# Two attention blocks and a SwiGLU layer on one core: moving columns taken from two halves in turn, and one more cast on VectorE

## The chip, the cores and the metric

The kernel runs on one core of a Trainium2 chip, in one launch. Time is device time in microseconds (us). Three runs of the kernel before took 1459.44 to 1459.61 us, with a median of 1459.46 us. PE is TensorE's matmul side and PEld its weight loads, DVE is VectorE, ACT is ScalarE, POOL is GpSimd, SP is the engine that issues the DMAs here.

## The reference

The input x has 4 batches of 12,416 tokens of 128 numbers. Attention runs twice: 32 inducing rows look at the tokens, which gives a summary h of 32 rows, and then every token looks at h. The result goes through a gated feed-forward layer with 1,536 inner units.

```
def mab(q, kv):
    s = scale * (q @ kv.transpose(0, 2, 1))
    a = np.exp(s - s.max(-1, keepdims=True))
    a /= a.sum(-1, keepdims=True) + 1e-09
    return a @ kv
h = mab(I, x)
attn = mab(x, h)                  # (4, 12416, 128)

g = attn @ w_gate                 # 49664 tokens, 128 -> 1536
val = attn @ w_val
out = (g / (1 + np.exp(-g)) * val) @ w_out
```

## The kernel before

**Columns and steps.** A batch's tokens are cut into 25 columns (`COLS`): 13 of 512 tokens and 12 of 480. Each column takes 12 steps (`NT`), one for each 128 of the 1,536 inner units. One step of one column is a slot, so there are 300 slots in a batch and 1,200 in all. The second attention's last product is folded into the weights: for each batch the kernel multiplies h with the gate and value weights once, in high and low parts, into a tile `tw` (`st.w`), and the moving operand of a column is then a tile `stack` that holds the token's 32 attention weights four times, as high and low parts, which SP's DMAs put there (`spread`, L499).

**One slot.** `front` makes the gate and the value product, two PE matmuls (L691, L692) that both read the same `stack` tile as moving operand, into two PSUM tiles named `gv`. `gate` lets ACT take the silu of the first (L697). `value` lets DVE multiply it with the second (L705); the result h goes to a tile `h`, or back into the PSUM tile for steps 1, 5 and 9 (`DVE_TILES`). `split` makes two fp32r parts of h: the high part `h_hi` is a cast (L713), done by DVE where the step is in `CAST` and by ACT elsewhere; the low part `h_lo` is the difference (L715), done by DVE in the steps of `DVE_TILES` and by POOL elsewhere. `back` makes three matmuls for a step, into one PSUM tile `o` over the 12 steps of a column: `h_hi` with the low part of the output weights (L729), `h_hi` with the high part (L730), and `h_lo` with the high part (L731). After the last step `evac` lets DVE copy `o` out (L738) and SP store it (L740). The first column of the first batch is an exception (`whole`): its h stays in F32, and one F32 product of each step (L727) takes the place of the three.

**Order.** All instructions are written in one fixed order by the loop at L756. In a slot this is: the products of slot k; silu and multiplication of slot k; the split of slot k-1; whatever attention steps of the next batch are due at this slot; and then the three output products of a slot that lies some slots back. The list `pend` and the number `ahead` set how far back: 5 slots in quiet stretches (`SKEW`), up to 10 ahead of a burst (`HI`). In seven slots a burst comes (a long exponential on ACT), and there DVE casts whatever the step is. The attention of the next batch is spread by `plan` over the slots of this batch, so that only the first batch's attention, some 60 us, stands by itself. In the fourth batch nothing is interleaved but the finishing of its own columns.

**Buffers.** `stack` has 3 buffers, `silu` 2, `h` 3, `h_hi` 11, `h_lo` 10, and PSUM has 6 tiles `gv` and 2 tiles `o`. The tiles `stack`, `h_hi` and `h_lo` are 64 elements longer than a column (`WB`), and a column begins at an offset in them that `AT` sets: 16, 48 and 48 elements for the wide columns and 0, 32 and 16 for the narrow ones.

**The moving operand.** In all five products a matmul streams its n columns (512 or 480) in the order in which they lie in SBUF: `st.stack[c][:, :n]`, `u.hi[:, :n]`, `u.lo[:, :n]`. The output of each goes to PSUM in the same order, and the host puts the blocks of tokens back into place.

Of the kernel before, what the change touches and what calls it, by code (L numbers as in the profile page):

```python
# [17 lines left out]
B, N, C, M, DFF = 4, 12416, 128, 32, 1536  # L18
P = 128
NG = 4  # L20
NTB = N // NG // 32


def starts(sizes):
# [10 lines left out]
WF = 32 * max(FC)  # L35
WB = WF + 64
AT = (16, 48, 48), (0, 32, 16)
NT = DFF // P
# [14 lines left out]
WP = 512  # L53
# [1 line left out]
PC = 384  # L55
GA = 4
DVE_TILES = {1, 5, 9}
CAST = {11}
E0 = 36


# [44 lines left out]
def induced_set_attention_then_swiglu(ctx: ExitStack, tc: tile.TileContext, xt, xn, ind, wgv, wo, out):  # L106
    nc = tc.nc
# [44 lines left out]
    def wcol(k, t):  # L152
        at = WP * (t // 2) + 2 * P * k + P * (t % 2)
        return slice(at, at + P)

    wgv_sb = const.tile([P, 2 * DFF], F32, name="wgv_sb")
    wo_hi = const.tile([P, DFF], F32R, name="wo_hi")
    wo_lo = const.tile([P, DFF], F32R, name="wo_lo")
# [39 lines left out]
    def at(u):  # L198

        return AT[u > NG * FC.count(max(FC))]  # L200
# [10 lines left out]
    def attention(b, one, xn0=None, xt0=None):  # L211
# [5 lines left out]
        def psum(second=0):  # L217
            if xn0 is not None or second:
                return ps_gv.tile([P, 512], F32, name="gv")
            return ps_o.tile([P, 512], F32, name="o")  # L220
# [53 lines left out]
        def s1(q, second=0):  # L274
            if q == 0:
                st.s = one.tile([P, NTB * 32], F32, name="s_all")
                st.mx = att.tile([P, NCH], F32, name="mx")
# [84 lines left out]
        def hacc2(q):  # L362
            g = q >= GA
            n0, n1 = (0, CH0[GA])[g], (CH0[GA], NTB)[g]
            if q in (0, GA):
# [65 lines left out]
        def sl2(b0, b1):  # L431
            return st.s2[:, b0:b1, :]

        def s2_m(b0, b1, second=0):
            if not hasattr(st, "s2"):
                st.s2 = one.tile([P, NTB, M], F32, name="s_all")
            st.sp[b0] = psum(second)
# [16 lines left out]

        def exp2(b0=0, b1=NTB):
            nc.scalar.activation(out=sl2(b0, b1), in_=sl2(b0, b1), func=AF.Exp)
# [166 lines left out]
    start = tc.manual_schedule()  # L623
    start.__enter__()
    s_all = oneb.tile([P, NTB * 32], F32, name="s_all")
    with tc.tile_pool(name="xt0", bufs=NCH - NXT) as xt0, tc.tile_pool(name="xn0", bufs=NCH - NXN) as xn0:
        cur = attention(0, one, xn0, xt0)
        f = cur.f
# [3 lines left out]
        pieces = {}  # L632
# [11 lines left out]
        def run(token):  # L644
            name, *args = token.split(":")
            args = [int(x) if x.isdigit() else x for x in args]
            if name == "ld":
                load_piece(*args)
            elif args and args[0] in pieces:
                getattr(pieces[args[0]], name)(*args[1:])  # L650
            else:
                short[name](*args)
# [27 lines left out]
    def front(st, b, c, t):  # L680
        u = Tile()
        q, j = COLS[c]
        u.b, u.q, u.j, u.t = b, q, j, t
        u.at = at(c)
        n = u.n = WF if q == 0 else 32 * FC[q]

        u.whole = b == 0 and c == 0
        rhs = st.stack[c][:, :n]
        u.g = ps_gv.tile([P, 512], F32, name="gv")
        u.v = ps_gv.tile([P, 512], F32, name="gv")  # L690
        nc.tensor.matmul(out=u.g[:, :n], lhsT=st.w[:, wcol(0, t)], rhs=rhs, start=True, stop=True)  # L691
        nc.tensor.matmul(out=u.v[:, :n], lhsT=st.w[:, wcol(1, t)], rhs=rhs, start=True, stop=True)  # L692
        return u
# [5 lines left out]
    def value(u):  # L699
        n = u.n  # L700
        if u.whole:
            u.h = hip.tile([P, WB], F32, name="h_hi")[:, :WF]
        else:
            u.h = u.v if u.t in DVE_TILES else hp.tile([P, WF], F32, name="h")
        nc.vector.tensor_mul(out=u.h[:, :n], in0=u.v[:, :n], in1=u.s[:, :n])  # L705
# [13 lines left out]
    def back(u):  # L719
        n, t = u.n, u.t  # L720
        if t == 0:
            acc["o"] = ps_o.tile([P, 512], F32, name="o")
        o = acc["o"]
        ws = slice(P * t, P * t + P)
        if u.whole:
            k = t % (WP // P)
            nc.tensor.matmul(out=o[:, :n], lhsT=pieces[f"o{t // (WP // P)}"].w[:, P * k:P * k + P], rhs=u.h[:, :n], start=(t == 0), stop=(t == NT - 1))  # L727
        else:
            nc.tensor.matmul(out=o[:, :n], lhsT=wo_lo[:, ws], rhs=u.hi[:, :n], start=(t == 0), stop=False)  # L729
            nc.tensor.matmul(out=o[:, :n], lhsT=wo_hi[:, ws], rhs=u.hi[:, :n], start=False, stop=False)  # L730
            nc.tensor.matmul(out=o[:, :n], lhsT=wo_hi[:, ws], rhs=u.lo[:, :n], start=False, stop=(t == NT - 1))  # L731
        if t == NT - 1:
            evac(u, o)

    def evac(u, o):
        n = u.n
        ob = obp.tile([P, WF], F32, name="ob")
        nc.vector.tensor_copy(out=ob[:, :n], in_=o[:, :n])  # L738
        at = NG * 32 * FC0[u.q] + u.j * n
        nc.sync.dma_start(out=out[u.b, P * at:P * (at + n)].rearrange("(d t) -> d t", d=P), in_=ob[:, :n])  # L740
# [6 lines left out]
    def first(t):  # L747
        made.append(front(cur, 0, 0, t))
        pend.append(made[t])

    short |= dict(f=first, g=lambda t: gate(made[t]), m=lambda t: value(made[t]), k=lambda t: back(pend.pop(0)))
    for token in SECOND.split():
        run(token)
    cur.steps = [(slot, lambda token=token: run(token)) for slot, tokens in FIRST.items() for token in tokens.split()]
    ahead = len(pend)
    for b in range(B):  # L756
        nxt = attention(b + 1, (one, oneb)[(b + 1) % 2]) if b + 1 < B else None
        if nxt is not None:
            nxt.steps = plan(nxt, PA if b == 0 else PB)
            if b == 0:  # L760
                cur.steps.append((nxt.e1, lambda: run(f"e2:52:{NTB}")))
                for q in range(2, NF):
# [6 lines left out]
        for slot in range(NT if b == 0 else 0, SLOTS):  # L769
            c, t = slot // NT, slot % NT  # L770
            u = front(cur, b, c, t)
            gate(u)
            value(u)
            u.cast_dve = t in CAST
            u.last = b == B - 1 and slot == SLOTS - 1
            if wait:
                split(wait[0])
                pend.append(wait.pop(0))
            wait.append(u)
            if slot in bursts:  # L780
                u.cast_dve = True
                split(u)
                pend.append(wait.pop(0))
            for a in (cur, nxt):
                while a is not None and a.steps and a.steps[0][0] <= slot:

                    if pend and pend[0].t in getattr(a.steps[0][1], "acc", ()):
                        break
                    a.steps.pop(0)[1]()
            ahead = min(ahead + 1 / RAMP, HI) if nxt is not None and slot < last_burst else max(ahead - 1 / RAMP, SKEW)  # L790
            if slot in bursts:
                ahead = SKEW - (b == 0)
            while len(pend) + len(wait) > ahead:
                back(pend.pop(0))
# [5 lines left out]
    for u in pend + wait:  # L800
        back(u)
# [37 lines left out]
```

## Time and profile before

| | before |
|---|---|
| median of 3 runs | 1459.46 us |
| the profiled execution, its span | 1459.38 us, 1457.6 us |
| PE busy | 1446.8 us (99%) |
| ACT busy | 1278.5 us (88%) |
| POOL busy | 1208.5 us (83%) |
| DVE busy | 1195.6 us (82%) |
| granted TensorE clock | 1.000 |
| share of PE in the chain that ended last | 94% |

The span is what the profiler sees of the instructions; 1.8 us of the execution's time lie around it. A matmul's busy time is longer than its turn: one follows the next before the first has ended, so the turn (from one start to the next) has to be read from a timeline and not from a mean duration. Granted clock 1.000 means that TensorE was never slowed. The chain of work that ended last follows the execution backwards from its last instruction, each time to what released it.

### The profile page before, as it was taken

How to read it: one execution, taken by the hardware profiler on the slowest of the kernel's cores; microseconds unless marked ns; L12 is line 12 of the kernel's file. 1: busy time of each engine (PE TensorE's matmuls, PEld its weight loads, DVE VectorE, ACT ScalarE, POOL GpSimd, SP SyncE). 2: the span in 40 equal slices, each digit the busy share in tenths (PEclk: the TensorE clock that was granted, in tenths of full speed). 3: DMA queues.
4: the chain of work that ended last, by engine and by line, in shares of the span. 5: the costliest groups of instructions: out<-in, count | busy, mean ns of one | idle time of the engine just before them, and what ended most of it. 6: DMA issues, size and time to landing. Idle time of an engine off the chain costs nothing.

```text
span 1457.6 us, 24926 instructions
## 1 busy us (share of the span) xinstructions
PE 1446.8 (99%) x7452; PEld 1174.3 (81%) x7452; DVE 1195.6 (82%) x2080; ACT 1278.5 (88%) x2388; POOL 1208.5 (83%) x995
## 2 busy tenths in 40 slices
PE   8999999999999999999999999999999999999999
PEld 5577788788887787888888788688888888888887
DVE  6888778887888789888788778987878878878877
ACT  5888898799998887998989888799899999999997
POOL 1689778888998778888899868878889889988987
PEclk9999999999999999999999999999999999999999
DMA  9234522221144242211123522221111111111110
GB/s 370 66 99 127 182 74 99 103 66 54 45 134 138 79 136 105 75 46 41 35 68 114 185 86 87 105 79 42 35 36 41 44 37 37 44 35 40 37 41 21
DMA packets 50822, 119.80 MB, mean 82 GB/s; under 512 B 11392, under 2 KB 28288, under 8 KB 50688
## 3 DMA queue, kind: packets, MB, share of 16 engines
q1 hardware_dynamic: 50688, 118.22, 24.8%
q8 instruction: 59, 0.97, 0.3%
q14 instruction: 75, 0.61, 0.1%
HBM read 62.87 MB, written 25.43 MB: 61 GB/s over the span
## 4 chain that ended last, share of the span: by engine, by line
PE 94%; ACT 2%; DMA 2%; POOL 1%; issue 1%; DVE 0%; SPq 0%; ACTq 0%; DVEq 0%
PE gv L691 18%; PE o L729 18%; PE gv L692 18%; PE o L731 18%; PE o L730 18%; PE gv L270 2%; PE o L318 1%; DMA s_all<-wgv 1%; DMA xt<-xt 1%; PE o L270 1%; PE o L727 1%; ACT silu L697 1%; POOL h_lo L715 1%; ACT h_hi L713 0%; PE gv L420 0%
## 5 line engine op out<-in xcount | busy, mean ns | idle before, releaser
L715 POOL TENSOR_TENSOR h_lo<-h,h_hi 128x512 fp32r<-128x512 f32 (+1 forms) x890 | 1113.2, 1276 | 202.4 <-ACT h_hi L713 142.4
L697 ACT ACTIVATE silu<-gv 128x512 f32<-128x512 f32 (+1 forms) x1200 | 704.2, 588 | 112.5 <-PE gv L691 73.5
L705 DVE TENSOR_TENSOR h<-gv,silu 128x512 f32<-128x512 f32 (+1 forms) x891 | 594.2, 668 | 194.5 <-ACT silu L697 143.8
L713 ACT CAST h_hi<-h 128x512 fp32r<-128x512 f32 (+1 forms) x788 | 475.2, 603 | 29.8 <-DVE h L705 24.6
L691 PE MATMUL gv<-stack,tw 128*128 128x512 f32 (+1 forms) x1200 | 469.0, 391 | 2.0 <-DVE stack L543 1.3
L692 PE MATMUL gv<-stack,tw 128*128 128x512 f32 (+1 forms) x1200 | 463.2, 386 | 0.6 <-ACT silu L697 0.4
L729 PE MATMUL o<-h_hi,wo_lo 128*128 128x512 f32 (+1 forms) x1188 | 460.8, 388 | 0.0
L731 PE MATMUL o<-h_lo,wo_hi 128*128 128x512 f32 (+1 forms) x1188 | 457.6, 385 | 0.0
L730 PE MATMUL o<-h_hi,wo_hi 128*128 128x512 f32 (+1 forms) x1188 | 455.3, 383 | 0.0
L729 PEld LDWEIGHTS o<-h_hi,wo_lo 128*128 128x128 f32 x1188 | 222.6, 187 | 53.9 <-issue 12.1
L691 PEld LDWEIGHTS gv<-stack,tw 128*128 128x128 f32 x1200 | 225.3, 188 | 48.5 <-ACT tw L412 2.6
L692 PEld LDWEIGHTS gv<-stack,tw 128*128 128x128 f32 x1200 | 225.8, 188 | 47.1 <-ACT silu L697 4.0
L731 PEld LDWEIGHTS o<-h_lo,wo_hi 128*128 128x128 f32 x1188 | 223.1, 188 | 42.6 <-POOL h_lo L715 0.4
L730 PEld LDWEIGHTS o<-h_hi,wo_hi 128*128 128x128 f32 x1188 | 223.1, 188 | 41.1
L705 DVE TENSOR_TENSOR gv<-gv,silu 128x512 f32<-128x512 f32 (+1 forms) x297 | 201.7, 679 | 40.5 <-ACT silu L697 39.3
L715 DVE TENSOR_TENSOR h_lo<-gv,h_hi 128x512 fp32r<-128x512 f32 (+1 forms) x297 | 197.5, 665 | 1.8 <-ACT h_hi L713 0.2
L713 ACT CAST h_hi<-gv 128x512 fp32r<-128x512 f32 (+1 forms) x294 | 167.4, 570 | 10.0 <-DVE gv L705 8.8
L738 DVE COPY ob<-o 128x512 f32<-128x512 f32 (+1 forms) x100 | 66.4, 664 | 0.8 <-PE o L731 0.8
L713 DVE CAST h_hi<-h 128x512 fp32r<-128x512 f32 (+1 forms) x103 | 60.6, 589 | 0.0
L483 POOL TENSOR_TENSOR a_lo<-aT,a_hi 128x480 fp32r<-128x480 f32 (+2 forms) x26 | 32.6, 1253 | 0.0
L190 POOL TENSOR_TENSOR wgv_sb<-s_all 128x512 int32<-128x512 int32 x2 | 2.9, 1456 | 28.8 <-ACT s_all L178 28.8
L467 POOL TENSOR_TENSOR s_all<-s_all,sm 128x512 f32<-128x512 f32 (+2 forms) x27 | 26.1, 967 | 0.0
(155 smaller groups left out, 476.5 us busy)
## 6 DMA issues: line engine op xcount, KB each, us to landing
xt_sb<-xt SPq DMA_DIRECT2D x32, 896.0 KB, 5.3
xn_sb<-xn SPq DMA_DIRECT2D x18, 896.0 KB, 5.9
out<-ob SPq DMA_DIRECT2D x52, 256.0 KB, 2.0
out<-ob SPq DMA_DIRECT2D x48, 240.0 KB, 2.0
stack<-a_hi SPq DMA_DIRECT2D x96, 64.0 KB, 2.0
stack<-a_lo SPq DMA_DIRECT2D x96, 64.0 KB, 2.0
stack<-a_hi SPq DMA_DIRECT2D x96, 60.0 KB, 2.0
stack<-a_lo SPq DMA_DIRECT2D x96, 60.0 KB, 2.0
```

The lines of the kernel that those rows point to most:

```text
L270: nc.tensor.matmul(out=ps[32 * j:32 * j + 32, 32 * (lo - b0):32 * (hi - b0)], lhsT=lhsT, rhs=st.xt[q][:, lo - CH0[q]:hi - CH0[q], j, :], s ...
L483: eng.tensor_sub(out=st.al[q][:, :n], in0=st.at[q][:, :n], in1=st.ah[q][:, :n].bitcast(F32))
L691: nc.tensor.matmul(out=u.g[:, :n], lhsT=st.w[:, wcol(0, t)], rhs=rhs, start=True, stop=True)
L692: nc.tensor.matmul(out=u.v[:, :n], lhsT=st.w[:, wcol(1, t)], rhs=rhs, start=True, stop=True)
L697: nc.scalar.activation(out=u.s[:, :u.n], in_=u.g[:, :u.n], func=AF.Silu)
L705: nc.vector.tensor_mul(out=u.h[:, :n], in0=u.v[:, :n], in1=u.s[:, :n])
L713: (nc.vector.tensor_copy if u.cast_dve else nc.scalar.copy)(out=u.hi[:, :n], in_=u.h[:, :n])
L715: eng.tensor_sub(out=u.lo[:, :n], in0=u.h[:, :n], in1=u.hi[:, :n].bitcast(F32))
L729: nc.tensor.matmul(out=o[:, :n], lhsT=wo_lo[:, ws], rhs=u.hi[:, :n], start=(t == 0), stop=False)
L730: nc.tensor.matmul(out=o[:, :n], lhsT=wo_hi[:, ws], rhs=u.hi[:, :n], start=False, stop=False)
L731: nc.tensor.matmul(out=o[:, :n], lhsT=wo_hi[:, ws], rhs=u.lo[:, :n], start=False, stop=(t == NT - 1))
L738: nc.vector.tensor_copy(out=ob[:, :n], in_=o[:, :n])
```

## The change

A helper `turns` gives a view of the same n columns in another order: column 0, column n/2, column 1, column n/2 + 1, and so on. The view has two dimensions beside the partition: n/2 positions one element apart, and within each the two halves, n/2 elements apart (256 elements or 1,024 bytes in a wide column, 240 elements or 960 bytes in a narrow one). The five products of a slot, and the F32 product of the first column, read their moving operand through it. The outputs are written to PSUM as before, one column after the other, so h lies in turned order; the output product turns it once more, and the host undoes both turns with one permutation of every block. No buffer, DMA, offset or weight changes.

Step 3 joins step 11 in `CAST`: DVE makes `h_hi` of step 3, ACT no longer does.

```diff
+def turns(x):
+
+    return x.rearrange("p (a b) -> p b a", a=2)
...
-CAST = {11}
+CAST = {3, 11}
...
-        rhs = st.stack[c][:, :n]
+        rhs = turns(st.stack[c][:, :n])
...
-            nc.tensor.matmul(out=o[:, :n], lhsT=pieces[f"o{t // (WP // P)}"].w[:, P * k:P * k + P], rhs=u.h[:, :n], start=(t == 0), stop=(t == NT - 1))
+            nc.tensor.matmul(out=o[:, :n], lhsT=pieces[f"o{t // (WP // P)}"].w[:, P * k:P * k + P], rhs=turns(u.h[:, :n]), start=(t == 0), stop=(t == NT - 1))
         else:
-            nc.tensor.matmul(out=o[:, :n], lhsT=wo_lo[:, ws], rhs=u.hi[:, :n], start=(t == 0), stop=False)
-            nc.tensor.matmul(out=o[:, :n], lhsT=wo_hi[:, ws], rhs=u.hi[:, :n], start=False, stop=False)
-            nc.tensor.matmul(out=o[:, :n], lhsT=wo_hi[:, ws], rhs=u.lo[:, :n], start=False, stop=(t == NT - 1))
+            hi, lo = turns(u.hi[:, :n]), turns(u.lo[:, :n])
+            nc.tensor.matmul(out=o[:, :n], lhsT=wo_lo[:, ws], rhs=hi, start=(t == 0), stop=False)
+            nc.tensor.matmul(out=o[:, :n], lhsT=wo_hi[:, ws], rhs=hi, start=False, stop=False)
+            nc.tensor.matmul(out=o[:, :n], lhsT=wo_hi[:, ws], rhs=lo, start=False, stop=(t == NT - 1))
...
-        blk = o[:, P * NG * 32 * c0:P * NG * 32 * (c0 + c)]
+        n = WF if c0 == 0 else 32 * c
+        turn = np.arange(n).reshape(2, n // 2).T.reshape(-1)
+        back = np.argsort(turn[turn])
+        blk = o[:, P * NG * 32 * c0:P * NG * 32 * (c0 + c)].reshape(B, -1, P, n)[..., back]
```

## The prediction

> **What bounds the kernel now.** The page comes first: busy time, the slices and the chain of work that ended last.
>
> ```profile
> span 1457.6 us, 24926 instructions
> PE 1446.8 (99%) x7452; PEld 1174.3 (81%) x7452; DVE 1195.6 (82%) x2080; ACT 1278.5 (88%) x2388; POOL 1208.5 (83%) x995
> ...
> PE   8999999999999999999999999999999999999999
> ...
> PE 94%; ACT 2%; DMA 2%; POOL 1%; issue 1%; DVE 0%; SPq 0%; ACTq 0%; DVEq 0%
> ```
>
> PE is busy in every slice, and 94% of the chain is PE following itself. So the time is the number of products times the turn of one, and only a shorter or longer turn moves it. The timeline of PE gives the turns: quiet stretches of the fourth batch (wide, then narrow columns) and of the first batch's narrow columns.
>
> ```profile
> 1200.07 0.39 PE L691 MATMUL gv<-stack,tw 128*128 128x512 f32 x1
> ...
> 1202.34 0.39 PE L691 MATMUL gv<-stack,tw 128*128 128x512 f32 x1
> ```
> ```profile
> 1400.32 0.38 PE L691 MATMUL gv<-stack,tw 128*128 128x480 f32 x1
> 1400.54 0.38 PE L692 MATMUL gv<-stack,tw 128*128 128x480 f32 x1
> 1400.76 0.38 PE L729 MATMUL o<-h_hi,wo_lo 128*128 128x480 f32 x1
> 1400.98 0.38 PE L730 MATMUL o<-h_hi,wo_hi 128*128 128x480 f32 x1
> 1401.19 0.38 PE L731 MATMUL o<-h_lo,wo_hi 128*128 128x480 f32 x1
> 1401.41 0.38 PE L691 MATMUL gv<-stack,tw 128*128 128x480 f32 x1
> ```
> ```profile
> 350.05 0.38 PE L691 MATMUL gv<-stack,tw 128*128 128x480 f32 x1
> ...
> 352.20 0.38 PE L691 MATMUL gv<-stack,tw 128*128 128x480 f32 x1
> ```
>
> Between the two wide rows lie ten products: a wide slot takes 2.27 / 2 = 1.135 us, 0.227 us a product. A narrow slot takes 1.09 us, 0.218 a product, and in the first batch 2.15 / 2 = 1.075. With a sixteenth fewer columns a narrow product should take 0.213 if columns set its time, and one amount of work takes 1.09 in one stretch and 1.075 in another. So a turn holds something beside the columns themselves.
>
> Is there room below? The only other product of this shape is the first column's F32 one, which goes in two passes.
>
> ```profile
> 50.74 1.02 PE L727 MATMUL o<-h_hi,s_all 128*128 128x512 f32 x2
> ```
> ```profile
> L727 PE MATMUL o<-h_hi,s_all x16: 590/592/592, 50.7 to 60.6; 128*128 128x512 f32 x16
> ```
>
> The first fence is the timeline, which merges the two passes; the second is the list of this line's instructions. Two passes of 0.592 us each end 1.02 us after the first began, so the second began 0.43 us later. I read the F32 pass as taking two ticks for a column where the fp32r product takes one (an estimate: no row shows the tick). Then 512 columns at one tick are 0.215 us, and the fp32r turn has 0.012 us over it. Is that the weight load beside it? One place speaks against it:
>
> ```profile
> 209.21 0.39 PE L691 MATMUL gv<-stack,tw 128*128 128x512 f32 x1
> 209.41 0.19 PEld L692 LDWEIGHTS gv<-stack,tw 128*128 128x128 f32 x1 [0.24 <-ACT silu L697]
> 209.43 0.48 PE L692 MATMUL gv<-stack,tw 128*128 128x512 f32 x1
> ```
>
> Here the next weights began to load 0.20 us into the product, and the next product still stands 0.22 to 0.23 behind it. So the excess belongs to the streaming of the moving operand or to the product itself; the change touches the first.
>
> **The turned read, part by part.** It removes no instruction and adds none: 3,084 wide products (624 slots of two, 612 of three) and 2,880 narrow ones (576 slots of five) read the same bytes in another order. No row of before has a moving operand that jumps at every column, so its turn has to be bounded from both sides.
>
> Lower bound: the excess goes wholly. A wide slot becomes 5 x 0.215 = 1.075 us and a narrow one 1.075 x 480 / 512 = 1.008. The gains are 612 x (1.135 - 1.075) = 36.7 us, 480 x (1.09 - 1.008) = 39.4 and 96 x (1.075 - 1.008) = 6.4 (first batch), together 82.5 us. Upper bound: each column is read by itself and costs what it costs in the F32 pass, 0.43 us for 512. Slots become 2.15 and 2.016 us: 612 x 1.015 + 480 x 0.926 + 96 x 0.941 = 621.2 + 444.5 + 90.3 = 1156 us more.
>
> I take the lower end. What decides for me is that the narrow turn isn't one number: from row to row it is 0.22, 0.22, 0.22, 0.21, 0.22, its sum differs between batches, and L729 and L730, which differ in these rows, stream the same h_hi. An excess that changes while bytes, count and operand stay the same is a matter of which addresses meet which, and order of reading changes just that. A fixed toll per product would be the same everywhere.
>
> [...]
>
> **Step 3's cast.** 99 casts (100 columns less the first, which isn't split) go from ACT to DVE. The stretches have their cost:
>
> ```profile
> 1130.00:1290.00 160.00, 160.00 (x707) 132.53 (x706) 131.10 (x216) 147.97 (x271) 142.49 (x112) 1.00 0.13 40
> 1305.00:1445.00 140.00, 140.00 (x642) 120.31 (x641) 113.81 (x192) 126.93 (x246) 121.10 (x101) 1.00 0.11 34
> ```
>
> (The columns are stretch, PE, PEld, DVE, ACT, POOL, clock, DMA.) The groups of L713 in these two stretches, and the waits of the whole span:
>
> ```profile
> L713 ACT CAST h_hi<-h 128x512 fp32r<-128x512 f32 x95 | 58.4, 614 | 2.0 <-DVE h L705 1.7
> ...
> L713 DVE CAST h_hi<-h 128x512 fp32r<-128x512 f32 x12 | 5.0, 420 | 0.0
> ...
> L713 DVE CAST h_hi<-h 128x480 fp32r<-128x480 f32 x11 | 6.6, 600 | 0.0
> ```
> ```profile
> POOL h_lo L715 <- DVE h_hi L713: 16.1, 30, 1.5
> ...
> POOL h_lo L715 <- ACT h_hi L713: 142.4, 216, 8.2
> ```
>
> ACT loses 99 x 0.6 = about 59 us, DVE gains 99 x 0.42 to 0.60 = 42 to 59. On DVE the cast stands behind the multiplication of step 4; behind it stand the multiplication of step 5, and on POOL the low part of step 3. PE needs that low part some five slots later, 5 us, so with PE at its present turn the cast costs nothing. Without that cover it would cost POOL's wait, 16.1 / 30 = 0.54 us each.
>
> **What is late next.** The wide stretch has 141 slots, the narrow one 128. POOL is busy 142.49 / 141 = 1.01 us and 121.10 / 128 = 0.95 us of a slot, DVE 0.93 and 0.89 (0.97 and 0.94 with another twelfth of a cast), ACT 1.05 and 0.99 (1.00 and 0.94 with a cast less). All lie below the new PE slots of 1.075 and 1.008, POOL by 0.06. But POOL also idles 17.5 / 141 = 0.124 and 18.9 / 128 = 0.148 us of a slot, mostly behind casts. If this idling shrinks as needed, the cost is 0. If half of it stays, and each moved cast adds 0.54 / 12 = 0.045, POOL's slots are 1.01 + 0.062 + 0.045 = 1.117 and 0.95 + 0.074 + 0.045 = 1.069, and the gains shrink to 612 x 0.018 + 480 x 0.021 + 96 x 0.006 = 11 + 10 + 1 = 22 us. Between 0 and 60 us given back I take 25, nearer to the first: five slots of lead are there to lend.
>
> **Sum.** Against the profiled execution: 1459.4 - 82.5 + 25 = 1402 us. That execution lies 0.1 us under the median, so nothing is added.
>
> **The rivals.** *The upstream engines set the pace.* PE quickens, and POOL, fed by two casts of DVE, becomes the bound: 1459.4 - 22 = 1437 us. For it: 0.06 us of room a slot. Against it: POOL's wait for ACT's casts, 142.4 us, is idleness PE's pace allowed.
>
> *The order of reading doesn't matter.* The excess is a toll of each fp32r product, or reading is the same speed in any order. Then only the cast moves, under cover: 1459 us. For it: the wide turn is 0.227 at every place that I looked at. Against it: the narrow turns.
>
> *Every column pays for its jump: slower.* [...] At the F32 pass's pace that is 1459.4 + 1156 = 2615 us. It decides from the point at which a column costs more than now, 0.227 / 512 = 0.44 ns. For it: all moving operands of before are neighbours in runs of 32 or more, so the trace has no sign that jumps are free. [...]
>
> **Chances.** The forecast 0.52 (1402, itself 1375 to 1420), POOL's pace 0.15 (1420 to 1450), no matter 0.13 (1455 to 1464), the jump 0.20. The range 1374 to 1465 holds the first three. A difference under 0.2%, 3 us, can't be told from none. Faster: 0.52 + 0.15 = 0.67; same 0.12; slower 0.20 plus 0.01 of the third case.
>
> **What would show it.** If the forecast holds, the timeline's wide turn is near 0.215 us and the narrow one near 0.202, alike in all batches; PE's share of busy time falls below 99% with waits for h_lo; DVE has 99 casts more in L713 and ACT as many fewer. If POOL sets the pace, the turns shorten and PE stands idle ahead of L731 behind L715. If order doesn't matter, turns stay at 0.227 and 0.218. If the jump costs, they are 0.4 or more and ACT, DVE and POOL idle half the time. The forecast is wrong if wide and narrow turns move unlike (1,024 and 960 bytes are different distances), or if the excess sits in the product and not in its read.

## The result and the profile after

The changed kernel takes 1417.3 us (median of 4 runs, 1416.7 to 1418.6) against 1459.5 us: a ratio of 0.971, with a 95% interval of 0.9693 to 0.9727. The forecast was 1402 us, so it is faster, by 42 us where 57 were expected.

The page of the kernel after, first its span and busy times, then its chain of waits:

```profile
span 1415.2 us, 25083 instructions
...
PE 1394.7 (99%) x7452; PEld 1173.8 (83%) x7452; DVE 1239.0 (88%) x2179; ACT 1202.5 (85%) x2289; POOL 1194.5 (84%) x995
...
PE 81%; ACT 6%; DVE 5%; issue 4%; POOL 4%; DMA 0%; DVEq 0%; ACTq 0%; POOLq 0%
```

PE's share of the chain fell from 94% to 81%: ACT, DVE and POOL now stand in it with 15% together. The timeline of PE after, in the fourth batch's wide and in its narrow columns:

```profile
1200.15 0.38 PE L696 MATMUL gv<-stack,tw 128*128 128x512 f32 x1
...
1202.31 0.38 PE L696 MATMUL gv<-stack,tw 128*128 128x512 f32 x1
...
1307.62 0.37 PE L696 MATMUL gv<-stack,tw 128*128 128x480 f32 x1
...
1308.63 0.37 PE L696 MATMUL gv<-stack,tw 128*128 128x480 f32 x1
```

A wide slot takes 2.16 / 2 = 1.08 us here (1.135 before) and a narrow one 1.01 (1.09). From one start to the next, with pauses left out, a wide product now takes 215.9 ns (227.3 before) and a narrow one 202.6 (217.9); the narrow turn is 202 or 203 ns at the median for each of the five products and in every batch. These means are worked out from all starts in the trace. So the turned read gave 3,084 x 11.4 ns + 2,880 x 15.3 ns = 79 us, and the question is where 79 - 42 = 37 us of it went. The starts show most of it as longer pauses: what PE takes from one product of a slot to the next beyond the turn adds up to 12 us before and to 46 us after. Five waits, first in the kernel before, then in the kernel after:

```profile
ACT h_hi L713 <- DVE h L705: 24.6, 54, 0.8
POOL h_lo L715 <- DVE h_hi L713: 16.1, 30, 1.5
...
ACT h_hi L713 <- DVE gv L705: 8.8, 14, 1.2
...
PEld gv L692 <- ACT silu L697: 4.0, 13, 0.8
...
PEld o L731 <- POOL h_lo L715: 0.4, 1, 0.4
```
```profile
POOL h_lo L720 <- DVE h_hi L718: 64.6, 106, 4.5
...
ACT h_hi L718 <- DVE gv L710: 55.5, 86, 1.4
...
ACT h_hi L718 <- DVE h L710: 26.4, 65, 0.6
...
PEld gv L697 <- ACT silu L702: 25.0, 69, 0.8
PEld o L737 <- POOL h_lo L720: 17.4, 41, 0.8
```

ACT's casts wait 55.5 + 26.4 = 82 us for DVE's multiplications, where the two rows were 8.8 and 24.6 us before, 33 us together. Behind ACT the weight loads of PE wait for silu (25.0 us, 4.0 before), and behind POOL for h_lo (17.4 us, 0.4 before).

One place shows how it comes about. The timeline after, in a narrow column of the fourth batch:

```profile
1326.41 0.64 DVE L210 TENSOR_REDUCE pairs<-s_all 128x15 f32<-128x480 f32 x1
...
1327.20 0.66 DVE L710 TENSOR_TENSOR h<-gv,silu 128x480 f32<-128x480 f32 x1
1327.77 0.24 DVE L468 RECIPROCAL sm<-sm 128x15 f32<-128x15 f32 x1
1327.93 0.59 DVE L710 TENSOR_TENSOR h<-gv,silu 128x480 f32<-128x480 f32 x1
1327.95 0.57 ACT L702 ACTIVATE silu<-gv 128x480 f32<-128x480 f32 x1 [0.88 <-DVE h L710]
1328.44 0.40 DVE L718 CAST h_hi<-h 128x480 fp32r<-128x480 f32 x1
...
1328.75 0.65 DVE L744 COPY ob<-o 128x480 f32<-128x480 f32 x1
1328.98 1.21 POOL L720 TENSOR_TENSOR h_lo<-h,h_hi 128x480 fp32r<-128x480 f32 x1 [0.87 <-DVE h_hi L718]
...
1330.07 0.56 ACT L718 CAST h_hi<-gv 128x480 fp32r<-128x480 f32 x1 [0.44 <-DVE gv L710]
...
1330.15 1.00 POOL L472 TENSOR_TENSOR s_all<-s_all,sm 128x480 f32<-128x480 f32 x1
...
1331.15 0.19 PEld L697 LDWEIGHTS gv<-stack,tw 128*128 128x128 f32 x1 [0.26 <-ACT silu L702]
...
1332.37 0.19 PEld L737 LDWEIGHTS o<-h_lo,wo_hi 128*128 128x128 f32 x1 [0.72 <-POOL h_lo L720]
```

In slot 4 of a column (slots are counted from 0, as steps are) DVE has its multiplication, step 3's cast (1328.44) and the copy of the finished column before (1328.75), one after another, and here the steps that prepare a coming column (1326.41, 1327.77) stand just ahead. ACT waits 0.44 us for the late product, POOL 0.87 us for the cast, and PE's weight loads 0.26 us at 1331.15 and 0.72 us at 1332.37. The place shows two causes at once: ACT had waited 0.88 us behind the preparing steps already (1327.95), and POOL makes one of these steps itself (1330.15) before it gets to the low parts that PE waits for.

### The profile page after: what moved, and what is told of

It reads as the page before. It is cut to its first block, busy times and chain, and to the rows that moved or that the text cites. A ratio compares the mean times of both kernels' runs of the same rounds, so it can differ in the third digit from the quotient of the medians.

```text
span 1415.2 us, 25083 instructions
## 1 busy us (share of the span) xinstructions
PE 1394.7 (99%) x7452; PEld 1173.8 (83%) x7452; DVE 1239.0 (88%) x2179; ACT 1202.5 (85%) x2289; POOL 1194.5 (84%) x995
## 4 chain that ended last, share of the span: by engine, by line
PE 81%; ACT 6%; DVE 5%; issue 4%; POOL 4%; DMA 0%; DVEq 0%; ACTq 0%; POOLq 0%
PE gv L697 15%; PE o L737 15%; PE gv L696 15%; PE o L735 15%; PE o L736 14%; ACT silu L702 3%; POOL h_lo L720 2%; DVE h L710 2%; PE gv L275 2%; ACT h_hi L718 2%; PE o L323 1%; POOL s_all L472 1%; PE o L732 1%; DVE h_hi L718 1%; DVE gv L710 1%
## 5 line engine op out<-in xcount | busy, mean ns | idle before, releaser
L720 POOL TENSOR_TENSOR h_lo<-h,h_hi 128x512 fp32r<-128x512 f32 (+1 forms) x890 | 1099.0, 1259 | 173.0 <-ACT h_hi L718 72.0
L697 PE MATMUL gv<-stack,tw 128*128 128x512 f32 (+1 forms) x1200 | 454.4, 379 | 4.6 <-ACT silu L702 3.4
L696 PE MATMUL gv<-stack,tw 128*128 128x512 f32 (+1 forms) x1200 | 454.6, 379 | 3.6 <-ACT silu L702 1.6
L718 ACT CAST h_hi<-h 128x512 fp32r<-128x512 f32 (+1 forms) x689 | 420.9, 611 | 39.1 <-DVE h L710 26.4
L737 PE MATMUL o<-h_lo,wo_hi 128*128 128x512 f32 (+1 forms) x1188 | 447.1, 376 | 4.7 <-POOL h_lo L720 4.1
L735 PE MATMUL o<-h_hi,wo_lo 128*128 128x512 f32 (+1 forms) x1188 | 445.5, 375 | 0.0
L736 PE MATMUL o<-h_hi,wo_hi 128*128 128x512 f32 (+1 forms) x1188 | 442.8, 373 | 0.0
L737 PEld LDWEIGHTS o<-h_lo,wo_hi 128*128 128x128 f32 x1188 | 224.4, 189 | 41.6 <-POOL h_lo L720 17.4
L718 ACT CAST h_hi<-gv 128x512 fp32r<-128x512 f32 (+1 forms) x294 | 169.4, 576 | 58.1 <-DVE gv L710 55.5
L718 DVE CAST h_hi<-h 128x512 fp32r<-128x512 f32 (+1 forms) x202 | 118.2, 586 | 0.0
```

The costliest lines, as they stand in the source:

```text
L718: (nc.vector.tensor_copy if u.cast_dve else nc.scalar.copy)(out=u.hi[:, :n], in_=u.h[:, :n])
L720: eng.tensor_sub(out=u.lo[:, :n], in0=u.h[:, :n], in1=u.hi[:, :n].bitcast(F32))
L735: nc.tensor.matmul(out=o[:, :n], lhsT=wo_lo[:, ws], rhs=hi, start=(t == 0), stop=False)
L736: nc.tensor.matmul(out=o[:, :n], lhsT=wo_hi[:, ws], rhs=hi, start=False, stop=False)
L737: nc.tensor.matmul(out=o[:, :n], lhsT=wo_hi[:, ws], rhs=lo, start=False, stop=(t == NT - 1))
```

## Experiments

Each kernel is timed beside the kernel before on the same chip; the latter's median was 1459.6 to 1459.8 us each time. Edits are shown against the changed kernel unless the text says otherwise.

### The turned read alone

```diff
-CAST = {3, 11}
+CAST = {11}
```

> The turned read alone; step 3's cast goes back to ACT. Theory A (the cast relieves ACT, which has 0.99 us of work for a narrow slot of 1.012 us without it): turns stay at 0.216 and 0.2025 us, the time goes up from 1417 to 1422-1430 us, and PE waits longer for silu. Theory B (the cast costs more on DVE than it saves on ACT, because a DVE cast that starts beside a POOL subtraction takes up to 2.5 us and ACT's casts of steps 4 and 5 then wait for DVE): 1404-1412 us, and ACT's waits for DVE's multiplications fall from 82 us to about 35.

1397.3 us (1396.9 to 1399.1), ratio 0.9576 (0.9562 to 0.959). Theory A fell and theory B had the direction, though the time lies 7 us below its range: without step 3's cast on DVE the kernel is 20 us faster than the changed kernel. By batch the 20 us are 5.3, 4.5, 4.7 and 5.2, so the cast costs alike in all four. The waits of this run:

```profile
DVE h L710 <- ACT silu L702: 85.7, 229, 3.1
...
ACT h_hi L718 <- DVE h L710: 34.5, 71, 0.8
...
PEld gv L697 <- ACT silu L702: 9.6, 27, 0.8
PEld o L737 <- POOL h_lo L720: 8.9, 30, 0.5
...
ACT h_hi L718 <- DVE gv L710: 5.0, 9, 1.2
```

ACT's waits for DVE are 39.5 us, near the 33 of the kernel before, and of the two waits of PE's weight loads one fell to about half and the other to 0.4. The turns are the same (216 and 203 ns), and PE's pauses between products add up to 26 us.

### The cast alone

The kernel before with `CAST = {3, 11}`.

> Step 3's cast on DVE alone, moving columns in their own order. Theory A: PE's turn of 0.227 and 0.218 us covers the cast, so the time is that of before within 3 us, and DVE's casts go from 106 to some 205. Rival (the cast is part of the gain): 1440-1450 us.

1462.2 us (1461.0 to 1463.7), ratio 1.0017 (1.0007 to 1.0027). It is within the 3 us of theory A, but the interval leaves zero out: even at PE's old turn the cast costs about 2.7 us. It was no part of the gain. The casts in this run (three more come in bursts, 205 in all):

```profile
L713 DVE CAST h_hi<-h x202: 394/418/2577, 63.0 to 1455.6; 128x512 fp32r<-128x512 f32 x53, 128x480 fp32r<-128x480 f32 x48
```

### Twelve orders of reading in one kernel

The front products of a column take one of twelve views of `stack`, by the column's number (the first column of a batch keeps the turned one); the output products read in turned order throughout. The tokens of a block stay in the order in which they were read.

```diff
-        nc.tensor.matmul(out=u.g[:, :n], lhsT=st.w[:, wcol(0, t)], rhs=rhs, start=True, stop=True)
-        nc.tensor.matmul(out=u.v[:, :n], lhsT=st.w[:, wcol(1, t)], rhs=rhs, start=True, stop=True)
+        x = st.stack[c][:, :n]
+        k = 12 if c == 0 else (c - 1) % 12
+        if k == 0:
+            y = x
+            nc.tensor.matmul(out=u.g[:, :n], lhsT=st.w[:, wcol(0, t)], rhs=y, start=True, stop=True)
+            nc.tensor.matmul(out=u.v[:, :n], lhsT=st.w[:, wcol(1, t)], rhs=y, start=True, stop=True)
...
+        if k == 1:
+            y = x.rearrange("p (a b) -> p b a", a=2)
...
+        if k == 4:
+            y = x.rearrange("p (a b c) -> p b a c", a=2, c=2)
...
+        if k == 8:
+            y = x.rearrange("p (g a b) -> p g b a", a=2, b=4)
...
+        if k == 11:
+            y = x.rearrange("p (g a b) -> p g b a", a=4, b=4)
...
```

> The two front products of each column read the stack tile in one of twelve orders, by column; the output products read in turned order. The tokens of a block are left in the order in which they were read, so the output is permuted. What counts is the start-to-start turn of the gate product, wide and narrow, by order. Theory A (two streams in turn suffice, however near): every order that goes to another 16-byte line at each column gives 0.216 and 0.2025 us, also with the two streams 16 to 64 bytes apart; the contiguous order 0.227 and 0.22. Theory B (it is the distance, pieces of 64 bytes or more): partners 8 to 32 bytes apart stay at 0.22 or more, halves and quarters give 0.216 and 0.2025. [...]

Here only the turns count, the median start-to-start times of the gate product and the value product (48 of each per order and width), worked out from the trace:

| order | wide, ns | narrow, ns |
|---|---|---|
| as they lie | 238, 233 | 221, 215 |
| two streams 8 bytes apart (0, 2, 1, 3, within four neighbours) | 238, 233 | 219, 215 |
| two streams 16 bytes apart | 216, 216 | 203, 202 |
| two streams 32 bytes apart | 216, 216 | 203, 203 |
| two streams 64 bytes apart | 216, 216 | 202, 203 |
| two halves, one column in turn (the change) | 216, 216 | 202, 203 |
| two halves, two columns in turn | 328, 333 | 297, 308 |
| two halves, four columns in turn | 243, 254 | 226, 228 |
| two halves, sixteen columns in turn | 239, 240 | 227, 224 |
| four streams 16 bytes apart | 265, 269 | 248, 252 |
| four quarters | 267, 282 | 250, 255 |
| eight eighths | 525, 510 | 392, 408 |

The timeline of this run, the gate product and what follows it, for columns as they lie, halves in turn, halves two columns at a time, and streams 16 bytes apart:

```profile
1166.42 0.40 PE L700 MATMUL gv<-stack,tw 128*128 128x512 f32 x1
1166.66 0.40 PE L701 MATMUL gv<-stack,tw 128*128 128x512 f32 x1
...
1179.61 0.38 PE L704 MATMUL gv<-stack,tw 128*128 128x512 f32 x1
1179.83 0.38 PE L705 MATMUL gv<-stack,tw 128*128 128x512 f32 x1
...
1229.10 0.50 PE L716 MATMUL gv<-stack,tw 128*128 128x512 f32 x1
1229.43 0.51 PE L717 MATMUL gv<-stack,tw 128*128 128x512 f32 x1
...
1286.74 0.38 PE L732 MATMUL gv<-stack,tw 128*128 128x512 f32 x1
1286.96 0.38 PE L733 MATMUL gv<-stack,tw 128*128 128x512 f32 x1
```

0.24, 0.22, 0.33 and 0.22 us. Theory A holds for two streams: all pairs tried that lie 16 bytes or more apart and are read one column in turn take 216 ns in a wide column, at 16 bytes as at 1,024. For four and eight streams, which go on to another 16 bytes at each column too, it fails: 265 to 282 ns and 510 to 525. A swap inside four neighbours, two streams 8 bytes apart, changes little or nothing (238 and 233 ns, as they lie 238 and 233). Theory B fell: partners 16 and 32 bytes apart take 216 ns too. Taking two neighbours at a time is the slowest of the two-stream orders, 328 and 333 ns; four and sixteen at a time take 239 to 254. The whole run took 1500.4 us, 83 more than the changed kernel; by the table the slow orders add some 105 us to the products.

### Other offsets in the kernel before

```diff
-AT = (16, 48, 48), (0, 32, 16)
+AT = (16, 48, 48), (16, 48, 48)
```

> The kernel before with the narrow columns' tiles at the wide ones' offsets (16, 48, 48 elements in place of 0, 32, 16). Theory A (the excess is a matter of which addresses follow each other): the narrow turns, now 0.213 to 0.223 us by product, change by some ns each, and the time with them, 1445-1475 us. Rival (a fixed toll of each fp32r product): narrow turns as before, 1459 us within 3.

1456.0 us (one run). The narrow turns did change. In most columns one product takes 212 ns and the next 221, whichever of the five it is, and in others all take 215 to 218 (the first narrow column of a batch apart); the mean is 216.7. Before, they had been 213 to 223 by product, with a mean of 217.9. 2,880 x 1.2 ns = 3.5 us, as measured. So the excess of the old order depends on where the tiles begin, and a toll that is the same for every product, here 212 ns for one and 221 for the next, is ruled out. In the mean, though, these offsets moved only 1.2 of the 15 ns that the turned read takes away.

### Where does the cast's price come from?

Three kernels with the turned read and other steps in `CAST`.

```diff
-CAST = {3, 11}
+CAST = {7, 11}
```

> Turned read, and the second DVE cast is that of step 7 in place of step 3. Two theories on the 20 us that step 3's cast costs. Theory P (its place: it is written into slot 4, where DVE also copies the finished o of the column before, so the multiplication of step 5 comes late, ACT's cast of step 5 waits for it, and the next silu): step 7's cast stands in a slot without a copy, so 1392-1402 us, and ACT's waits for DVE's multiplications stay near 40 us. Theory L (its load: DVE cannot take another 58 us at this pace, wherever it stands): 1412-1420 us.

1409.8 us (1409.6 to 1410.1), ratio 0.9656 (0.9642 to 0.9671): between the two theories. As many casts as in the changed kernel, put two slots behind the subtraction of step 5 and four behind the copy, cost 12.5 us where step 3's cost 20.

The second has `CAST = {3}`.

> Turned read, and the only DVE cast is that of step 3; ACT takes step 11's. DVE and ACT have as many casts as with step 11 alone (1397 us). Theory P (place): 1405-1418 us. Theory L (load): 1395-1400 us.

1416.1 us (1415.9 to 1418.7), ratio 0.9705 (0.9689 to 0.9721). DVE has as many casts as in the run with step 11 alone, and it takes 19 us longer. Here DVE's load is the same and the place is what differs. The casts themselves are not longer (0.42 us at the median in both runs). Its waits:

```profile
ACT h_hi L718 <- DVE gv L710: 40.1, 73, 1.2
...
PEld gv L697 <- ACT silu L702: 27.4, 74, 0.8
```

The third has an empty `CAST`.

> Turned read, no DVE cast but those of the bursts. If ACT has room for all casts, DVE's freedom gives 1385-1395 us. If ACT does not (0.99 us a narrow slot with eleven casts of twelve, 1.04 with twelve, against PE's 1.012), it becomes the bound in the narrow columns: 576 slots x 0.03 = 17 us more than with step 11's cast on DVE, 1410-1420 us, with PE waiting for silu.

1398.9 us (1398.5 to 1399.3), ratio 0.9582 (0.9567 to 0.9596). Neither end: ACT with all casts isn't the bound, and DVE without them gains nothing. ACT's busy time is 1292.7 us of a span of 1397.6, 92%. My estimate of its load, 1.04 us a narrow slot, came from its busy time at the slower pace and was too high: in the fourth batch's narrow columns it is 0.99 us. This run also shows that step 11's cast is free on either engine (1397.3 and 1398.9 us), so the 17 to 19 us of the run before belong to step 3's.

### The lead of the output products

```diff
-SKEW = 5
+SKEW = 7
...
-CAST = {3, 11}
+CAST = {11}
```

> Turned read, step 11's cast alone on DVE, and the output products follow seven slots behind in quiet stretches in place of five. 1397 us is some 19 us over what the turns alone would give (1378). If these are short waits of PE for late low parts, a longer lead takes them up: 1388-1393 us, PE's waits for h_lo near 0. If they are waits ahead of the gate and value products, for silu and PSUM tiles, the lead does nothing: 1396-1399 us.

1424.0 us (1423.1 to 1424.7), ratio 0.9753 (0.9739 to 0.9768): 27 us slower than with five slots, which neither expectation had. The order of the loop says where DVE's operations then stand in a column: with five slots of lead the copy of o is in slot 4; with seven it is in slot 6, beside the subtraction of step 5. That is again three DVE operations in one slot. Three more runs tested it.

The changed kernel (`CAST = {3, 11}`) with six slots, which puts the copy into slot 5:

> The changed kernel with the output products six slots behind in place of five, which moves DVE's copy of o from slot 4 to slot 5, away from step 3's cast. Theory P (three DVE operations in one slot are what costs): of the 20 us that step 3's cast costs, the place's part comes back, 1400-1410 us (the run with steps 7 and 11, where nothing coincides, had 1410). Theory L (a longer lead is itself what cost 27 us with seven slots): slower than the changed kernel, 1425-1435 us.

1414.4 us (1413.5 to 1417.1), ratio 0.9695 (0.9679 to 0.9711). Theory L fell, but theory P's figure missed too: only 3 us came back. Cast, copy and subtraction now stand in slots 4, 5 and 6, one extra operation in each of three slots on end. That this is nearly as bad as two extra in one is a reading after the fact, which no run tested by itself.

The turned read with step 11's cast and nine slots, which puts the copy into the empty slot 8:

> Turned read, step 11's cast alone on DVE, output products nine slots behind: DVE's copy falls into slot 8, where it has nothing but its multiplication (with seven slots it fell into slot 6, beside the subtraction of step 5, and the time was 1424 us). Theory P: 1390-1400 us. Theory L (the longer lead keeps the h_hi and h_lo buffers and the engines wait for them): 1430-1450 us.

1411.8 us (1410.7 to 1412.6), ratio 0.9671 (0.9656 to 0.9685). Between the two; the table below splits it. And six slots:

> Turned read, step 11's cast alone on DVE, output products six slots behind: the copy falls into slot 5, ahead of the subtraction in slot 6. Theory P: no slot has three DVE operations, so near 1397 us, 1394-1402. Theory L (a longer lead costs): between 1397 and 1424, about 1410 us.

1398.5 us (1398.3 to 1398.7), ratio 0.958 (0.9566 to 0.9594), as theory P had it.

In the first three batches the lead climbs to ten ahead of each burst, and the copy wanders with it (in the second batch after the change it stands in slot 4 for 14 of 25 columns and in slot 9 for 8). In the fourth batch the lead stays and hardly anything is interleaved, so the schedule shows by itself there. Mean time of a slot in its wide columns (11 columns) and its narrow ones (10 columns), from the starts of the gate products:

| kernel | DVE's extra operations by slot | wide, us | narrow, us | in all, us |
|---|---|---|---|---|
| before | cast 0, sub 2, copy 4, sub 6, sub 10 | 1.133 | 1.093 | 1459.5 |
| after | and cast 4 | 1.109 | 1.034 | 1417.3 |
| turns alone | cast 0, sub 2, copy 4, sub 6, sub 10 | 1.084 | 1.019 | 1397.3 |
| casts 7, 11 | and cast 8 | 1.094 | 1.025 | 1409.8 |
| cast 3 | sub 2, copy and cast 4, sub 6, sub 10 | 1.099 | 1.031 | 1416.1 |
| no cast | sub 2, copy 4, sub 6, sub 10 | 1.080 | 1.018 | 1398.9 |
| lead 7 | cast 0, sub 2, sub and copy 6, sub 10 | 1.098 | 1.033 | 1424.0 |
| casts 3, 11, lead 6 | cast 0, sub 2, cast 4, copy 5, sub 6, sub 10 | 1.097 | 1.024 | 1414.4 |
| lead 6 | cast 0, sub 2, copy 5, sub 6, sub 10 | 1.079 | 1.013 | 1398.5 |
| lead 9 | cast 0, sub 2, sub 6, copy 8, sub 10 | 1.079 | 1.015 | 1411.8 |

Five turns of 215.9 and 202.6 ns are 1.080 and 1.013 us. With leads of six and nine PE hardly stands in the columns of this batch, so there a longer lead is no harm. Of the other kernels with turned reads, those with five extra operations a column are slow where two of them share a slot (cast 3, lead 7), and those with six are slow in every place tried. So load and place both count; the table doesn't price them apart. In this batch the changed kernel loses 5.2 us against the turns alone and lead 7 loses 5.8; lead 7's other 20 lie in the first three batches, where the table doesn't speak. What lead 9 loses, it loses there too (12 of 14 us). Its waits have long ones that the run with five slots doesn't have:

```profile
PEld gv L696 <- ACT silu L702: 12.4, 11, 4.6
```

A burst sets `ahead` back to `SKEW`, and PE lives on the slots in between while ACT makes its long exponential: five slots from ten to five, one from ten to nine. That would explain these waits, from the code; no run took it apart.

### Streams 16 bytes apart, no offsets

```diff
-    return x.rearrange("p (a b) -> p b a", a=2)
+    return x.rearrange("p (g a b) -> p g b a", a=2, b=4)
...
-AT = (16, 48, 48), (0, 32, 16)
+AT = (0, 0, 0), (0, 0, 0)
...
-CAST = {3, 11}
+CAST = {11}
...
```

The host's permutation follows the new order.

> Turned read, step 11's cast alone on DVE, but the two streams are 16 bytes apart (neighbouring groups of four columns) and all tiles begin at offset 0. If only the alternation between two lines counts and offsets have no part in it, turns are 0.216 and 0.2025 us and the time is 1397 within 3 us. If distance or offset still matters when all five products read so, turns are longer, 1405 us or more.

1395.5 us (1395.3 to 1395.8), ratio 0.956 (0.9545 to 0.9574). The turns are 216 and 203 ns: neither distance (16 bytes here, 1,024 and 960 in the changed kernel) nor offset matters here once two streams take turns. It has the lowest time here, below both the kernel before and the changed one; from the turned halves alone (0.9562 to 0.959) it can't be told.

## Why the prediction was right, and where it was off

**The bound and the room.** The turn of a product set the time, and the floor read out of the F32 product, 0.215 us for 512 columns, is what the turned read reached: 215.9 ns. The gain was put at 82.5 us and measured as 79: the two floors had been put 1 ns a product too low, and they and the old turns came from rows rounded to 10 ns. That the F32 pass takes two ticks a column was an assumption; half its 0.43 us fits the 215.9 ns, and no run shows the tick itself. The argument that chose the lower bound, that the old narrow turns vary with addresses, held: in the run with other offsets they varied otherwise, and in the changed kernel they don't vary.

**The choice between the bounds.** The runs settle it for this read. The twelve orders show 216 ns for a wide product where two streams at least 16 bytes apart give one column each in turn, and 328 ns where each of the two halves gives two neighbours in turn. No order of two streams reached the upper bound's 0.43 us; four streams took 265 to 282 ns, and only eight went past it.

**The step that failed** is "What is late next", with 25 us given back where 37 were. This error and the smaller one of the turns add up: 1417 lies only 3 us inside the upper end of the forecast's own case (1375 to 1420). The step took POOL as the engine to watch, by averages over a stretch, and let the cast cost nothing because five slots of lead lay before PE. DVE did take the predicted time for it (118.2 us of casts in place of 60.6, 42 to 59 us more were expected), but the place counted. Cast 3 alone against step 11's cast alone shows this with equal load, and the waits are in line with this path: DVE's late multiplications delay ACT's casts (82 us of waits, 33 before), these the silus and POOL's low parts, and these PE's weight loads (25.0 and 17.4 us, 4.0 and 0.4 before). What the place costs and what a sixth operation a column costs wherever it stands (12.5 us with steps 7 and 11) is not taken apart. Of the 37 us, step 3's cast cost 20 and the other 17 are in the run with the turns alone. Of these, 14 are longer pauses between PE's products (26 us against 12), nearly half of them in the first batch; I have no full account of their cause. The cover was not whole even at the old turn: 2.7 us.

**The rivals.** "The upstream engines set the pace" came nearest beside the forecast, with DVE in POOL's part: 1417 us lies below its 1437. "The order of reading doesn't matter" and "every column pays" are out for two streams; eight streams go past the price that the latter gave (0.43 us a wide product), with 0.51 to 0.53.

## What to carry to other kernels

Where fp32r products set the time and their turn is longer than half an F32 pass of the same width (here 227 ns, the pass 0.43 us), try to let the moving operand alternate column by column between two streams 16 bytes or more apart; here streams 16 bytes apart did as well as two halves (216 ns both), and no offsets had to be tuned (216 ns with all at 0). When PE gets faster, look at the engines slot by slot, not by averages: a cast that is free in one slot cost 17 to 20 us of 1,400 in another. A change of two edits should be timed edit by edit; here one of the two took back a third of the 62 us that the other gave.

## What the runs showed of the hardware that was not expected

For a wide gate product: two streams one column at a time, 216 ns; two columns at a time, 328; four at a time, 16 bytes, 243; sixteen at a time, 239; as they lie, 238 beside turned output products and 227 among products that all read straight on. Four streams cost 265 to 282 ns (gate and value product) and eight 510 to 525. So one column each from two streams 16 bytes or more apart is the single fast order found, and what in the reading hardware makes it so stays open: the traces show turns, not accesses. The turn of a contiguous read seems to depend also on what its neighbours read: the same order took 238 ns (value product 233) and 227 ns in two kernels that differ in the order of the output products.
